# A decode layer with a cached attention window: maxima and mask added to the scores by VectorE instead of by two 512-column products, and key copies taken in turn

## The chip, the cores and the metric

The kernel runs on one core of one Trainium2 chip. The metric is the time of one execution on the device in microseconds (us); lower is better. Before the change the median of three runs is 127.63 us (127.57 to 128.44).

The core has a matrix engine (TensorE, "PE" in the profile; its weight loads are listed as "PEld"), a vector engine (VectorE, "DVE"), a scalar engine (ScalarE, "ACT"), GpSimd ("POOL") and SyncE ("SP"), which here issues the loads. Each engine runs its own list of instructions in order and waits for others by semaphores. Products are written to PSUM, from which VectorE and ScalarE read.

## The reference

One new token for each of 8 sequences goes through a layer norm, and then through attention over a cached window and through a gated feed-forward block. All inputs are bf16. The shapes are those of the inputs: x is 8 x 512, the caches 8 sequences x 8 key heads x 4096 positions x 128, of which the last W = 1024 are used.

```python
xn = _layernorm(x)
q  = (xn @ wq)                     # 512 -> 32 heads x 128, 4 query heads to a key head
k, v = k_cache[:, :, Sk - W:], v_cache[:, :, Sk - W:]        # W = 1024
scores = einsum("bhqd,bhkd->bhqk", q, k) * 128 ** -0.5
o  = einsum("bhqk,bhkd->bhqd", softmax(scores), v)
s  = o.reshape(8, 1, 32 * 128) @ wo                          # -> 512
g  = silu((gelu(xn @ w_gate) * (xn @ w_up)) @ w_down)        # 512 -> 1792 -> 512
return x + s * g
```

The bulk of the data are the keys and values: 64 pairs of a sequence and a key head, each 1024 x 128 in keys and again in values, 33.6 MB of the 47.5 MB read.

## The kernel before, in words

**Stages.** First the loads are issued; then come the layer norm, the feed-forward block and the query projection, which fill the first 33 us; then attention with the output projection in it; then the gate, the sum and the store. In the first stage `keep_busy` (L233) puts idle products between the pieces of work.

**Loads.** All large loads are issued by SyncE, in the order of L163 to L177, into a ring of 16 buffers of 1 MB: the feed-forward weights, the query weights, the first two key sets, and then for each q the key set q + 2, the value set q, and after every second q a slice of the output weights. A load waits until its buffer in the ring has been read.

**Rounds.** A round, numbered q from 0 to 15, takes QG = 4 sequences b..b+3 of one key head: a key set and a value set of 1 MB each. A load (L117) puts the 4 x 1024 keys of a set on 128 partitions in NCS = 32 chunks of 128 keys. Every chunk holds keys of all four sequences, 32 each, and the sequence of a row is its partition modulo 4. All 128 keys of a chunk are multiplied with the 16 queries of the four sequences (QC = 16 = 4 sequences x 4 query heads), and what belongs to another sequence has to be masked away. A round is worked in four quarters of 8 chunks, i from 0 to 3, and the quarters of all rounds are numbered g = 4 q + i. The small constants `row_of` (4 x 128, which row is whose) and `other` (4 x 16, -1e30 for the queries of the other sequences, else 0) make that mask as a product with 4 rows.

**The steps of a quarter or round** (all names and lines are of the kernel before):
- `transposes(g)` (L363): 8 transpositions of 128 x 128 keys into one PSUM tile `kT_ps` (two of these exist), and copies into SBUF: columns 0 to 639 by VectorE into `kTa` (L375), columns 640 to 1023 by ScalarE into `kTb` (L377).
- `scores(g)` (L381): in the first quarter of a round the mask is written into the whole score tile `sc_ps` (128 x 512 fp32, one product of 512 columns, L386). Then 8 products of 16 columns add the scores (L397).
- `max_keys(q)` (L406): the maximum over the 32 chunks, per partition and query, by VectorE (L408).
- `max_all(q)` (L413): the 128 x 16 maxima are transposed by PE (L416, fp32), reduced and negated by VectorE (L418), and put on the diagonal of a 48 x 16 bf16 tile `diag` in two parts, a value and its rounding rest (L423, L426).
- `exponentials(q)` (L436): a product of ones with this tile, 512 columns (L437), adds minus the maxima to the scores in PSUM; ScalarE takes the exponential into `pT` (L446).
- `sums(q)` (L448), `values(g)` (L469) and `normalise(q)` (L485): the sums over positions by 8 products with ones, reduced and inverted by VectorE; 8 products per quarter of the values with `pT`; and the result times the inverted sum into `oT_all` (L487).
- `project(h)` (L498): 4 products of the output weights of one head.

**Order.** There is no planner; the order of every engine is that of the program's text, the loop at L512 to L535. In step (q, i) PE does the transpositions of the next quarter, the maxima of the round before (at i = 1), the scores of this quarter, the sums (at i = 0) and values of the round two before, the exponentials of the round before (at i = 2), and in every second round, at i = 2 and 3, the projection of two heads each. At a round's end come `normalise` of the round two before and `max_keys` of this one. The tail, after the last quarter's scores, has no transpositions and scores left.

Of the kernel before, what the change touches and what calls it, by code (L numbers as in the profile page):

```python
# [17 lines left out]
def kernel(  # L18
# [30 lines left out]

    nc = tc.nc
    ctx.enter_context(tc.manual_schedule())

# [4 lines left out]
    W = min(4096, max(256, Sk // 4))  # L59
    win0 = Sk - W  # L60
    F = B_w_gate.shape[1]
    P = nc.NUM_PARTITIONS
    NDC = D // P
    NFC = F // P
    NSC = W // P
    UPK = NDC // 2
    DNJ = NFC // 2
    inv_sqrt_dh = float(Dh) ** -0.5

    QG = 4  # L70
    NB = QG
    NCS = QG * NSC
    VC = 4
    AC = 3
    NRING = 16
    MASK = -1.0e30
    NG = Hkv * B
    NQ = NG // QG
    QC = QG * rep
# [3 lines left out]
    consts = ctx.enter_context(tc.tile_pool(name="consts", bufs=1))  # L83
# [3 lines left out]
    ring = ctx.enter_context(tc.tile_pool(name="ring", bufs=NRING))  # L87
    kT_pool = ctx.enter_context(tc.tile_pool(name="kT_pool", bufs=3))
    p_pool = ctx.enter_context(tc.tile_pool(name="p_pool", bufs=4))
    small = ctx.enter_context(tc.tile_pool(name="small", bufs=2))  # L90
    ps_misc = ctx.enter_context(tc.tile_pool(name="ps_misc", bufs=1, space=PSUM))
    ps_kT = ctx.enter_context(tc.tile_pool(name="ps_kT", bufs=2, space=PSUM))
    ps_sc = ctx.enter_context(tc.tile_pool(name="ps_sc", bufs=2, space=PSUM))
    ps_mx = ctx.enter_context(tc.tile_pool(name="ps_mx", bufs=1, space=PSUM))
# [77 lines left out]
    for q in range(NQ):  # L172
# [12 lines left out]
        out=ident,  # L185
        in_=ident,
# [22 lines left out]
    other = consts.tile([QG, QG, rep], BF16, name="other")  # L209
    nc.vector.memset(other, MASK)  # L210
    nc.gpsimd.affine_select(
        out=other,
        in_=other,
# [3 lines left out]
        pattern=[[1, QG], [0, rep]],  # L217
        channel_multiplier=-1,
    )

    LO = 32
    diag = []
    for i in range(2):
        t = consts.tile([LO + QC, QC], BF16, name=f"diag{i}")
        nc.vector.memset(t, 0.0)
        diag.append(t)
    eps_sb = consts.tile([B, 1], FP32, name="eps_sb")
    nc.vector.memset(eps_sb, 1e-5)

# [3 lines left out]
    def keep_busy(n):  # L233
# [12 lines left out]
        out=rstd, in_=mv[:, 1:2], func=ACT.Sqrt, bias=eps_sb, scale=1.0  # L246
# [4 lines left out]
        out=xhat,  # L251
        in0=x_sb,
        scalar1=mv[:, 0:1],
        scalar2=rstd[:, 0:1],
        op0=ALU.subtract,
        op1=ALU.mult,
# [90 lines left out]
    for k in range(NDC):  # L347
        for m in range(Hq):
# [4 lines left out]
                start=(k == 0 and m == 0),  # L353
                stop=(k == NDC - 1),
                skip_group_check=True,
# [2 lines left out]
    nc.vector.tensor_copy(out=qT_all, in_=qT_ps.rearrange("p h b -> p b h"))  # L358


    kT, sc, pT, mxs, shift, recip = {}, {}, {}, {}, {}, {}

    def transposes(g):  # L363
        q, i = divmod(g, NB)
        kT_ps = ps_kT.tile([P, W], BF16, name="kT_ps")
        for c in range(NSC):
            n = i * NSC + c
            nc.tensor.transpose(  # L368
                kT_ps[:, c * P : (c + 1) * P],
                k_sb[q][:, n * Dh : (n + 1) * Dh],  # L370
                ident,
            )
        own = (NSC - AC) * P
        ta = kT_pool.tile([P, own], BF16, name="kTa")
        nc.vector.tensor_copy(out=ta, in_=kT_ps[:, 0:own])  # L375
        tb = kT_pool.tile([P, W - own], BF16, name="kTb")
        nc.scalar.copy(out=tb, in_=kT_ps[:, own:])  # L377
        kT[g] = [ta[:, c * P : (c + 1) * P] for c in range(NSC - AC)]
        kT[g] += [tb[:, c * P : (c + 1) * P] for c in range(AC)]

    def scores(g):  # L381
        q, i = divmod(g, NB)
        hkv, b = divmod(q * QG, B)
        if i == 0:
            sc[q] = ps_sc.tile([P, NCS, QC], FP32, name="sc_ps")
            nc.tensor.matmul(  # L386
                sc[q],
                row_of.rearrange("g e s -> g (e s)"),
                other.rearrange("g s j -> g (s j)")
                .unsqueeze(1)  # L390
                .to_broadcast([QG, NCS, QC]),
                start=True,
                stop=False,
                skip_group_check=True,
            )
        for c in range(NSC):
            nc.tensor.matmul(  # L397
                sc[q][:, i * NSC + c, :],
                kT[g][c],
                qT_all[:, b : b + QG, hkv * rep : (hkv + 1) * rep],  # L400
                start=False,
                stop=False,
                skip_group_check=True,
            )

    def max_keys(q):  # L406
        mx = small.tile([P, QC], FP32, name="mx")
        nc.vector.tensor_reduce(  # L408
            out=mx, in_=sc[q].rearrange("p c n -> p n c"), axis=AX.X, op=ALU.max
        )  # L410
        mxs[q] = mx

    def max_all(q):  # L413

        mxT_ps = ps_mx.tile([QC, P], FP32, name="mxT_ps")
        nc.tensor.transpose(mxT_ps, mxs[q], ident_f)  # L416
        nm = small.tile([QC, 1], FP32, name="nm")
        nc.vector.tensor_reduce(  # L418
            out=nm, in_=mxT_ps, axis=AX.X, op=ALU.max, negate=True
        )  # L420
        eye = ident_f[0:QC, 0:QC]
        parts = diag[q % 2]
        nc.vector.tensor_scalar(  # L423
            out=parts[0:QC, :], in0=eye, scalar1=nm[:, 0:1], scalar2=None, op0=ALU.mult
        )
        nc.vector.scalar_tensor_tensor(  # L426
            out=parts[LO : LO + QC, :],
            in0=eye,
            scalar=nm[:, 0:1],
            in1=parts[0:QC, :],  # L430
            op0=ALU.mult,
            op1=ALU.subtract,
        )
        shift[q] = parts

    def exponentials(q):  # L436
        nc.tensor.matmul(  # L437
            sc[q],
            ones_pp[0 : LO + QC, :],
            shift[q].unsqueeze(1).to_broadcast([LO + QC, NCS, QC]),  # L440
            start=False,
            stop=True,
            skip_group_check=True,
        )
        pT[q] = p_pool.tile([P, NCS, QC], BF16, name="pT")
        nc.scalar.activation(out=pT[q], in_=sc[q], func=ACT.Exp, scale=inv_sqrt_dh)  # L446

    def sums(q):  # L448
        sums_ps = ps_sum.tile([P, NB, QC], FP32, name="sums_ps")
# [60 lines left out]


    transposes(0)  # L512
    for q in range(NQ + LAG):
        v = q - LAG
        for i in range(NB):
            g = q * NB + i
            if g + 1 < NG:
                transposes(g + 1)
            if i == 1 and 1 <= q <= NQ:
                max_all(q - 1)  # L520
            if g < NG:
                scores(g)
            if v >= 0:
                if i == 0:
                    sums(v)
                values(v * NB + i)
            if i == 2 and 1 <= q <= NQ:
                exponentials(q - 1)
            if v >= SH and v % SH == 0 and i >= NB // 2:
                for h in range(2):  # L530
                    project((v // SH - 1) * rep + (i - NB // 2) * 2 + h)
        if v >= 0:
            normalise(v)
        if q < NQ:
            max_keys(q)  # L535
# [42 lines left out]
```

## Time and profile before

| | us |
|---|---|
| median of 3 runs | 127.63 (127.57 to 128.44) |
| the profiled execution, its own time | 127.63 |
| its span in the profile | 125.8 |
| PE busy in the span | 114.7 |
| VectorE busy | 64.5 |
| ScalarE busy | 42.5 |
| chain that ended last: PE's share | 73% |
| data read from HBM | 47.46 MB, 377 GB/s over the span |

The span runs from the first to the last instruction that the profile records; the execution's own time is 1.8 us more. A "busy" engine is one that has an instruction under way. Products overlap: a product that is listed with 0.2 us is followed by the next one after 0.03 to 0.06, so the time for which an instruction holds PE is read from the start of one to the start of the next, or from the chain, and not from its mean duration. The chain that ended last goes back from the last instruction to what released it, step by step, and gives the path that set the end. The slices cut the span in 40 parts of 3.1 us. The issue rows tell when a load is put on the queue; the median from there to its landing is 18.6 to 18.8 us for the keys and values.

### The profile page before, as it was taken

The numbers are of one execution on the slowest core, as the hardware profiler recorded it, in microseconds if no ns is written. First come the engines' busy times: TensorE is split into PE (matmuls) and PEld (weight loads), VectorE is DVE, ScalarE is ACT, GpSimd is POOL, SyncE is SP. The second block draws the span as 40 slices with busy tenths as digits, with TensorE's granted clock in tenths as the row PEclk, the third lists the DMA queues.
The fourth block names the chain that finished last, engine by engine and source line by source line (L and its number), as shares of the span: only waits on it lengthen the run. The fifth ranks groups of instructions, "written<-read, shape, count | busy, mean of one in ns | idle before, by whom it ended". The sixth has DMA issues, their size and how long they took to land.

```text
span 125.8 us, 4887 instructions
## 1 busy us (share of the span) xinstructions
PE 114.7 (91%) x2197; PEld 89.6 (71%) x2202; DVE 64.5 (51%) x200; ACT 42.5 (34%) x86; POOL 1.2 (1%) x7
## 2 busy tenths in 40 slices
PE   5899999989989999999999898989999999988780
PEld 1366663657777788887888787878787877877570
DVE  5200003010248768756786664858667677765531
ACT  4000005000054644543534254354544435352210
POOL 3000000000000000000000000000000000000000
PEclk9999999999999999999999999999999999999999
DMA  4999999999999999999999999999999999998300
GB/s 89 410 431 417 429 412 417 419 432 427 417 414 398 427 417 417 402 421 435 412 398 431 419 401 424 412 417 412 413 435 410 411 432 411 407 411 357 135 5 3
DMA packets 10325, 47.78 MB, mean 380 GB/s; under 512 B 816, under 2 KB 4928, under 8 KB 5696
## 3 DMA queue, kind: packets, MB, share of 16 engines
q1 hardware_dynamic: 10288, 47.46, 92.5%
q8 instruction: 17, 0.28, 0.9%
q14 instruction: 4, 0.03, 0.1%
q10 hardware_dynamic: 16, 0.01, 0.0%
HBM read 47.46 MB, written 0.01 MB: 377 GB/s over the span
## 4 chain that ended last, share of the span: by engine, by line
PE 73%; DVE 9%; ACT 6%; issue 5%; DMA 4%; ACTq 0%; DVEq 0%
PE kT_ps L368 19%; PE idle_ps L235 12%; PE o_ps L476 10%; PE sc_ps L397 9%; DVE kTa L375 6%; ACT kTb L377 6%; PE gu_ps L274 5%; DMA ring_sb<-in_B_w_gate_dram 4%; PE sc_ps L437 4%; PE sc_ps L386 4%; PE sT_ps L502 3%; PE sums_ps L451 3%; PE qT_ps L349 3%; PE fT_ps L313 1%; DVE mx L408 0%
## 5 line engine op out<-in xcount | busy, mean ns | idle before, releaser
L377 ACT COPY kTb<-kT_ps 128x384 bf16<-128x384 bf16 x64 | 30.6, 479 | 52.6 <-DVE kTa L375 52.6
L375 DVE COPY kTa<-kT_ps 128x640 bf16<-128x640 bf16 x64 | 31.3, 489 | 20.7 <-PE kT_ps L368 20.3
L368 PE MATMUL kT_ps<-ident,ring_sb 128*128 128x128 bf16 x512 | 39.1, 219 | 0.2 <-issue 0.2
L368 PEld LDWEIGHTS <-ring_sb 128*128 128x128 bf16 x512 | 29.4, 97 | 2.4 <-issue 2.2
L476 PE MATMUL o_ps<-pT,ring_sb 128*128 128x64 bf16 (+1 forms) x512 | 25.2, 190 | 2.2 <-issue 2.2
L235 PE MATMUL idle_ps<-ones_w 128*128 128x512 bf16 x53 | 20.0, 521 | 2.2 <-DVE ones_w L181 1.5
L476 PEld LDWEIGHTS <-ring_sb 128*128 128x128 bf16 x512 | 19.1, 97 | 3.0 <-issue 2.8
L397 PE MATMUL sc_ps<-qT_all,kTa 128*128 128x16 bf16 x320 | 17.8, 171 | 0.0
L397 PEld LDWEIGHTS <-kTa 128*128 128x128 bf16 x320 | 14.7, 96 | 4.2 <-issue 2.3
L397 PE MATMUL sc_ps<-qT_all,kTb 128*128 128x16 bf16 x192 | 14.5, 171 | 1.6 <-ACT kTb L377 0.4
L235 PEld LDWEIGHTS <-ones_w 128*128 128x128 bf16 x58 | 6.0, 121 | 8.8 <-issue 6.1
L397 PEld LDWEIGHTS <-kTb 128*128 128x128 bf16 x192 | 9.3, 96 | 3.3 <-ACT kTb L377 1.0
L408 DVE TENSOR_REDUCE mx<-sc_ps 128x16 f32<-128x512 f32 x16 | 10.9, 681 | 0.0
L446 ACT ACTIVATE pT<-sc_ps 128x512 bf16<-128x512 f32 x16 | 9.6, 601 | 2.7 <-PE sc_ps L437 2.6
L274 PEld LDWEIGHTS <-ring_sb 128*128 128x128 bf16 x112 | 7.4, 162 | 2.2 <-issue 1.6
L274 PE MATMUL gu_ps<-xnT_sb,ring_sb 128*128 128x8 bf16 x112 | 7.3, 201 | 0.5 <-DMA ring_sb<-in_B_w_gate_dram 0.5
L291 DVE TENSOR_SCALAR z<-z 128x112 f32<-128x112 f32 x1 | 0.2, 219 | 13.7 <-ACT z L288 13.7
L437 PE MATMUL sc_ps<-diag,ones_pp 48*128 48x512 bf16 x16 | 6.2, 386 | 0.4 <-DVE diag L426 0.4
L451 PE MATMUL sums_ps<-pT,ones_pp 128*128 128x64 bf16 x128 | 6.3, 192 | 0.0
L386 PE MATMUL sc_ps<-other,row_of 4*128 4x512 bf16 x16 | 6.2, 385 | 0.0
L502 PEld LDWEIGHTS <-wo_sb 128*128 128x128 bf16 x128 | 4.3, 96 | 2.5 <-issue 2.5
L502 PE MATMUL sT_ps<-oT_all,wo_sb 128*128 128x8 bf16 x128 | 5.4, 167 | 0.3 <-DVE oT_all L487 0.3
(54 smaller groups left out, 59.4 us busy)
## 6 DMA issues: line engine op xcount, KB each, us to landing
ring_sb<-in_A_k_cache_dram SPq DMA_DIRECT2D x16, 1024.0 KB, 18.8
ring_sb<-in_A_v_cache_dram SPq DMA_DIRECT2D x16, 1024.0 KB, 18.6
ring_sb<-in_A_wq_dram SPq DMA_DIRECT2D x4, 1024.0 KB, 19.5
wo_sb<-in_A_wo_dram SPq DMA_DIRECT2D x8, 512.0 KB, 17.8
ring_sb<-in_B_w_gate_dram SPq DMA_DIRECT2D x2, 896.0 KB, 5.0
ring_sb<-in_B_w_up_dram SPq DMA_DIRECT2D x2, 896.0 KB, 8.4
ring_sb<-in_B_w_down_dram SPq DMA_DIRECT2D x2, 896.0 KB, 12.9
x_sb<-in_A_x_dram ACTq DMA_DIRECT2D x1, 8.0 KB
```

What stands on the lines that cost most here:

```text
L235: nc.tensor.matmul(idle_ps, ones_w[:, 0:P], ones_w, start=True, stop=True)
L274: nc.tensor.matmul(ffn["gu"][:, j, n % 2, :], up_sb[n][:, i, j::NFC], xnT_sb[:, k, :], start=(n == 0 and j == 0 and i == 0), stop=(k == ND ...
L368: nc.tensor.transpose(kT_ps[:, c * P : (c + 1) * P], k_sb[q][:, n * Dh : (n + 1) * Dh], ident,)
L375: nc.vector.tensor_copy(out=ta, in_=kT_ps[:, 0:own])
L377: nc.scalar.copy(out=tb, in_=kT_ps[:, own:])
L386: nc.tensor.matmul(sc[q], row_of.rearrange("g e s -> g (e s)"), other.rearrange("g s j -> g (s j)") .unsqueeze(1) .to_broadcast([QG, NCS, ...
L397: nc.tensor.matmul(sc[q][:, i * NSC + c, :], kT[g][c], qT_all[:, b : b + QG, hkv * rep : (hkv + 1) * rep], start=False, stop=False, skip_g ...
L408: nc.vector.tensor_reduce(out=mx, in_=sc[q].rearrange("p c n -> p n c"), axis=AX.X, op=ALU.max)
L437: nc.tensor.matmul(sc[q], ones_pp[0 : LO + QC, :], shift[q].unsqueeze(1).to_broadcast([LO + QC, NCS, QC]), start=False, stop=True, skip_gr ...
L451: nc.tensor.matmul(sums_ps, ones_pp, pT[q][:, c * NB : (c + 1) * NB, :], start=(c == 0), stop=(c == NSC - 1),)
L476: nc.tensor.matmul(o_ps[q][:, 0:wide, :], v_sb[q][:, n * Dh : (n + 1) * Dh], pT[q][:, n : n + wide, :], start=(n == 0), stop=(n == NCS - 1 ...
L502: nc.tensor.matmul(sT_ps[0][:, d, :], wo_sb[:, h, d * P : (d + 1) * P], oT_all[:, h, :], start=(h == 0 and d == 0), stop=(h == Hq - 1), sk ...
```

## The change

Scores are no longer masked and shifted inside PSUM. The 512-column mask product goes from `scores`, whose products now each start anew. The maximum per partition is taken over unmasked scores; then `max_all` turns it with a plain fp32 product and adds the mask to the 16 x 128 result by a small product. A new function, `shift_all`, spreads the negated maxima over the 128 partitions with an fp32 product, adds the mask by a second small one, and copies the 128 x 16 result to SBUF; VectorE adds it to the 128 x 512 scores and writes the sum to SBUF, where the exponential reads it. The diagonal tiles and the 512-column product with them are gone. The keys of a quarter are copied whole, by VectorE for even i and by ScalarE for odd i. In the loop the value products stand ahead of the scores, and the three steps of the round before stand behind the scores at i = 0, 1 and 2.

```diff
     def transposes(g):
...
-        own = (NSC - AC) * P
-        ta = kT_pool.tile([P, own], BF16, name="kTa")
-        nc.vector.tensor_copy(out=ta, in_=kT_ps[:, 0:own])
-        tb = kT_pool.tile([P, W - own], BF16, name="kTb")
-        nc.scalar.copy(out=tb, in_=kT_ps[:, own:])
...
+        kT[g] = kT_pool.tile([P, W], BF16, name="kT")
+        if i % 2 == 0:
+            nc.vector.tensor_copy(out=kT[g], in_=kT_ps)
+        else:
+            nc.scalar.copy(out=kT[g], in_=kT_ps)

     def scores(g):
...
-            nc.tensor.matmul(
-                sc[q],
-                row_of.rearrange("g e s -> g (e s)"),
-                other.rearrange("g s j -> g (s j)")
-                .unsqueeze(1)
-                .to_broadcast([QG, NCS, QC]),
-                start=True,
-                stop=False,
-                skip_group_check=True,
-            )
...
-                start=False,
-                stop=False,
-                skip_group_check=True,
+                start=True,
+                stop=True,

     def max_all(q):
...
-        nc.tensor.transpose(mxT_ps, mxs[q], ident_f)
+        nc.tensor.matmul(mxT_ps, mxs[q], ident_f, start=True, stop=False)
+        nc.tensor.matmul(
+            mxT_ps,
+            other.rearrange("g s j -> g (s j)"),
+            row_of.rearrange("g e s -> g (e s)"),
+            start=False,
+            stop=True,
+        )
         nm = small.tile([QC, 1], FP32, name="nm")
         nc.vector.tensor_reduce(
             out=nm, in_=mxT_ps, axis=AX.X, op=ALU.max, negate=True
         )
-        eye = ident_f[0:QC, 0:QC]
-        parts = diag[q % 2]
-        nc.vector.tensor_scalar(
-            out=parts[0:QC, :], in0=eye, scalar1=nm[:, 0:1], scalar2=None, op0=ALU.mult
-        )
-        nc.vector.scalar_tensor_tensor(
...
-        shift[q] = parts
+        shift[q] = nm
+
+    def shift_all(q):
+
+        nm_ps = ps_mx.tile([P, QC], FP32, name="nm_ps", tag="mxT_ps")
+        nc.tensor.matmul(
+            nm_ps,
+            shift[q].to_broadcast([QC, P]),
+            ident_f[0:QC, 0:QC],
+            start=True,
+            stop=False,
+        )
+        nc.tensor.matmul(
+            nm_ps,
+            row_of.rearrange("g e s -> g (e s)"),
+            other.rearrange("g s j -> g (s j)"),
+            start=False,
+            stop=True,
+        )
+        to_add = small.tile([P, QC], FP32, name="to_add")
+        nc.vector.tensor_copy(out=to_add, in_=nm_ps)
+        shifted[q] = s_pool.tile([P, NCS, QC], FP32, name="shifted")
+        nc.vector.tensor_tensor(
+            out=shifted[q],
+            in0=sc[q],
+            in1=to_add.unsqueeze(1).to_broadcast([P, NCS, QC]),
+            op=ALU.add,
+        )

     def exponentials(q):
-        nc.tensor.matmul(
-            sc[q],
-            ones_pp[0 : LO + QC, :],
-            shift[q].unsqueeze(1).to_broadcast([LO + QC, NCS, QC]),
...
-        nc.scalar.activation(out=pT[q], in_=sc[q], func=ACT.Exp, scale=inv_sqrt_dh)
+        nc.scalar.activation(
+            out=pT[q], in_=shifted[q], func=ACT.Exp, scale=inv_sqrt_dh
+        )
...
             if g + 1 < NG:
                 transposes(g + 1)
-            if i == 1 and 1 <= q <= NQ:
-                max_all(q - 1)
-            if g < NG:
-                scores(g)
             if v >= 0:
                 if i == 0:
                     sums(v)
                 values(v * NB + i)
-            if i == 2 and 1 <= q <= NQ:
-                exponentials(q - 1)
+            if g < NG:
+                scores(g)
+            if 1 <= q <= NQ:
+                if i == 0:
+                    max_all(q - 1)
+                elif i == 1:
+                    shift_all(q - 1)
+                elif i == 2:
+                    exponentials(q - 1)
```

More of the change, by code (lines that the diff above doesn't have):

```diff
@@ L73 @@
     VC = 4
-    AC = 3
     NRING = 16
@@ L89 @@
     p_pool = ctx.enter_context(tc.tile_pool(name="p_pool", bufs=4))
+    s_pool = ctx.enter_context(tc.tile_pool(name="s_pool", bufs=2))
     small = ctx.enter_context(tc.tile_pool(name="small", bufs=2))
@@ L219 @@
     )
[L221 to L226, printed above, removed]
     eps_sb = consts.tile([B, 1], FP32, name="eps_sb")
@@ L358 @@
     nc.vector.tensor_copy(out=qT_all, in_=qT_ps.rearrange("p h b -> p b h"))
-    kT, sc, pT, mxs, shift, recip = {}, {}, {}, {}, {}, {}
+    kT, sc, pT, mxs, shift, shifted, recip = {}, {}, {}, {}, {}, {}, {}
     def transposes(g):
@@ L372, in transposes @@
             )
-        own = (NSC - AC) * P
-        ta = kT_pool.tile([P, own], BF16, name="kTa")
-        nc.vector.tensor_copy(out=ta, in_=kT_ps[:, 0:own])
-        tb = kT_pool.tile([P, W - own], BF16, name="kTb")
-        nc.scalar.copy(out=tb, in_=kT_ps[:, own:])
-        kT[g] = [ta[:, c * P : (c + 1) * P] for c in range(NSC - AC)]
-        kT[g] += [tb[:, c * P : (c + 1) * P] for c in range(AC)]
+        kT[g] = kT_pool.tile([P, W], BF16, name="kT")
[3 more added lines that the diff above has]
+            nc.scalar.copy(out=kT[g], in_=kT_ps)
     def scores(g):
@@ L398, in scores @@
                 sc[q][:, i * NSC + c, :],
-                kT[g][c],
+                kT[g][:, c * P : (c + 1) * P],
                 qT_all[:, b : b + QG, hkv * rep : (hkv + 1) * rep],
-                start=False,
-                stop=False,
-                skip_group_check=True,
+                start=True,
+                stop=True,
             )
@@ L420, in max_all, with exponentials @@
         )
-        eye = ident_f[0:QC, 0:QC]
-        parts = diag[q % 2]
-        nc.vector.tensor_scalar(
-            out=parts[0:QC, :], in0=eye, scalar1=nm[:, 0:1], scalar2=None, op0=ALU.mult
-        )
-        nc.vector.scalar_tensor_tensor(
[L427 to L432, printed above, removed]
-        )
-        shift[q] = parts
-    def exponentials(q):
+        shift[q] = nm
[7 more added lines that the diff above has]
+            stop=False,
+        )
         nc.tensor.matmul(
-            sc[q],
-            ones_pp[0 : LO + QC, :],
-            shift[q].unsqueeze(1).to_broadcast([LO + QC, NCS, QC]),
+            nm_ps,
+            row_of.rearrange("g e s -> g (e s)"),
+            other.rearrange("g s j -> g (s j)"),
             start=False,
             stop=True,
-            skip_group_check=True,
         )
+        to_add = small.tile([P, QC], FP32, name="to_add")
[7 more added lines that the diff above has]
+        )
+    def exponentials(q):
         pT[q] = p_pool.tile([P, NCS, QC], BF16, name="pT")
-        nc.scalar.activation(out=pT[q], in_=sc[q], func=ACT.Exp, scale=inv_sqrt_dh)
+        nc.scalar.activation(
+            out=pT[q], in_=shifted[q], func=ACT.Exp, scale=inv_sqrt_dh
+        )
     def sums(q):
```

## The prediction

> **What bounds the kernel now.** I read the page's slices first, then the chain of work that ended last, then the timeline. Two rows of the slices:
>
> ```profile
> PE 114.7 (91%) x2197; PEld 89.6 (71%) x2202; DVE 64.5 (51%) x200; ACT 42.5 (34%) x86; POOL 1.2 (1%) x7
> ...
> PEclk9999999999999999999999999999999999999999
> DMA  4999999999999999999999999999999999998300
> ```
>
> The loads run full from the second slice to the 36th, with nothing left to fill, and the matrix engine (PE) is busy beside them at its full clock. Which is later is read from the issue rows of the loads and the PE timeline. The last loads are issued at:
>
> ```profile
> 90.76 1.91 SPq L117 DMA_DIRECT2D ring_sb<-in_A_k_cache_dram  x1
> 93.25 1.86 SPq L117 DMA_DIRECT2D ring_sb<-in_A_v_cache_dram  x1
> ...
> 98.22 3.04 SPq L117 DMA_DIRECT2D ring_sb<-in_A_v_cache_dram  x2
> ```
>
> With the median of 18.6 to 18.7 us from issue to landing, the last key set (round 15) lands at 109.5 and value set 13 at 111.9. PE starts to transpose that key set at 110.2 and to use those values at 112.6. So at the end PE is only 0.7 us behind the loads; at round 3 (issued 20.3, so landed about 39.0; transposed from 46.1) it was 7 behind. PE sets the pace and the loads stand just ahead of it: a slower PE shows in full, a faster one gains less than a microsecond.
>
> The pace of PE, from the chain, round 3 (a round is one key set, one value of q, worked in four quarters):
>
> ```profile
> 47.47 0.32 PE sc_ps L386
> 47.79 0.29 PE sc_ps L397 x8
> 48.08 0.25 PE sums_ps L451 x8
> 48.33 0.23 PE o_ps L476 x8
> 48.56 0.46 PE kT_ps L368 x8
> ...
> 50.39 0.25 PE o_ps L476 x8
> 50.64 0.32 PE sc_ps L437
> ```
>
> From this mask product (L386) to the next at 52.38 it is 4.91 us, with PE busy for 4.86. Rounds with the output projection (every second one, 16 more products) take 5.3 to 5.5, and several have 0.3 to 0.5 of "issue" gaps in the midst of a group of products. These gaps wait for no engine in the trace; I leave them as they are.
>
> **The change, part by part, per round.**
>
> Removed from PE: the two 512-column products, 0.32 each on the chain (63.21 - 62.89 for L386), 0.64. The transposition of the maxima (L416) held PE from 59.42 to 59.53, 0.11. Together 0.75.
>
> The Trainium skill, "TensorE: Matmul & The Clock Gate", section "Back-to-back issue gap", gives N/2.4 + 2.5 ns, 216 ns for 512 columns. By that estimate only 0.43 + 0.11 would be removed and the body below would come out 2.7 us longer. The row (0.32, reload of the next weights included) decides.
>
> Added to PE: an fp32 product of the maxima with the identity, which is no transposition any more (128 columns, 16-column weights), a 128-column bf16 mask product, an fp32 product of the negated maximum (128-column weights, 16 columns) and a 16-column mask product. The bf16 pair costs as its neighbours: 0.06 for 128 columns (0.46 / 8, L368) and 0.04 for 16 (0.29 / 8, L397). No row shows a plain fp32 product. The nearest is the fp32 transposition, also 128 columns:
>
> ```profile
> 59.42 0.27 PE L416 MATMUL mxT_ps<-ident_f,mx 128*16 128x128 f32 x1
> 59.53 0.22 PE L397 MATMUL sc_ps<-qT_all,kTa 128*128 128x16 bf16 x3
> ```
>
> It occupied 0.11, twice a bf16 one (0.06). Least: the product costs as much as that, 0.11, and the 16-column one as a bf16 score, 0.04; with the masks 0.25. Most: four passes of 0.11, and four weight loads at the 0.12 of L235's load plus 0.04 each; with masks 0.44 + 0.64 + 0.10 = 1.18. I take two passes: 0.22, and two weight loads of 0.12 that hide nothing, with the columns and masks 0.38 in all, so 0.60. I choose it because the transposition, with one pass of fp32 at 0.11, is the nearest row, and both halves of two numbers have to go through.
>
> The same page of the skill (section "Terms") says that the transpose mode is 4 times faster for FP32. By it, as an estimate, the first product alone would be 0.44 and the sum 0.82; no row of the trace shows the pair, and the time would be 3 us longer.
>
> Key copies: VectorE took 640 columns, then ScalarE 384 of the same tile, one after the other:
>
> ```profile
> L377 ACT COPY kTb<-kT_ps 128x384 bf16<-128x384 bf16 x64 | 30.6, 479 | 52.6 <-DVE kTa L375 52.6
> L375 DVE COPY kTa<-kT_ps 128x640 bf16<-128x640 bf16 x64 | 31.3, 489 | 20.7 <-PE kT_ps L368 20.3
> ```
>
> From a tile's last transposition to its last copy was 0.02 + 0.50 + 0.08 + 0.49 + 0.05 = 1.14 (44.11 to 45.25). Whole copies: VectorE from the line through 174 ns at 32 columns (L263) and 489 at 640, 0.69; ScalarE from 198 ns at 32 columns (L325) and 479 at 384, 0.99, or 1.01 by the slope to 601 at 512. With 0.2 ahead and 0.05 behind, an even quarter's copy takes 0.94 and an odd one's 1.27. Since the value products now stand ahead of the scores, PE has, between the last transposition of a quarter and its scores, at least values 0.25, scores 0.29, transpositions 0.46, values 0.25 = 1.25. So the odd copies are hidden but for 0.02, and exactly at the edge: each 0.1 more there costs 0.1 in a round without projection.
>
> VectorE: out go two diagonal operations (0.22 each) and 4 x 0.49; in come 2 x 0.69, a small copy (0.17) and the addition over 512 fp32 from PSUM (the reduction L408 of that size takes 0.68, a two-operand row of 112 takes 0.27, which scales to 0.69). 3.60 busy in a round becomes about 3.5: no bound. ScalarE: 4 x 0.48 + 0.60 = 2.5 becomes 2 x 1.01 + 0.60 = 2.6, off the bound. The loads' queue and its order are untouched.
>
> New waits: the maxima's product now waits for the maximum in the open. Counting from the end of a round's first transpositions: copy 0.2 to 0.89, normalisation to 1.15, maximum 1.18 to 1.86, product at 1.91; PE gets there at 0.25 + 0.29 + 0.46 + 0.25 + 0.25 + 0.29 = 1.79. A stall of 0.12, with the next transpositions queued behind it. In rounds with projection 0.29 more work lies in between, and this stall and the 0.02 are gone. The second fp32 product waits for the negated maximum, 0.27 + 0.25 after the first; transpositions, values and scores (1.0) cover it.
>
> Body: 4.91 - 0.75 + 0.60 + 0.14 = 4.90 without projection; with it 5.5 - 0.15 = 5.35. Over the 13 rounds from 2 to 15 that is no change, to -0.9; I take 0 because of gaps that a hand count doesn't see.
>
> Start: in the first two rounds there are no values to cover the copies. Stepping through with 0.69, 1.01, 0.46 and 0.29: the scores of quarter 1 wait for ScalarE until 35.63, those of quarter 3 until 37.65, the first shift is ready at 41.5, and round 2's second transpositions start at 42.36 where they now start at 41.95. +0.4.
>
> End: from the last transposition of the last quarter (115.0) to the maximum at 117.16 was 2.13; now the copy on ScalarE 1.27, scores 0.29 + 0.17 to land, 0.03: 1.76, as the normalisation no longer stands in between. -0.4. From the start of the maximum to the last exponential was 2.31 (117.16 to 119.47). Now: maximum 0.73 with its hop, fp32 product and mask 0.49 (0.32 before, plus 0.17), reduction 0.33, second product and mask 0.48, small copy 0.22, addition 0.74 = 2.99. +0.7.
>
> Sum: 0 + 0.4 - 0.4 + 0.7 = +0.7. Span 125.8 + 0.7 = 126.5. The profiled execution took 127.63, 1.8 beyond its span, and equals the median of the runs shown: **128.3 us**. One per cent (1.3 us) is about what can be told from no change.
>
> **Rivals.**
>
> 1. Dear fp32 products (slower). Place: the two products in PE's queue, in every round. Price: each 0.1 over 0.60 is 1.3 us in the body and 0.1 in the tail; from about 0.65 it is over 128.9, and at 0.89, midway between my choice and the most, it is 0.29 x 14 = 4.1 more, 132.4. For it: nothing in the trace shows a plain fp32 product, and PE has nothing to give. Against: fp32 needs twice, not four times, in the one row there is. At the most (1.18) it would be 136.
>
> 2. The loads decide (X, the added PE time of a round, under 0.45). Then PE catches up and waits for value set 13 at 111.9: two groups of values (0.50), two of scores (0.58), two of transpositions (0.92) and both new pairs of products (0.3) later the last quarter's keys are transposed, at 114.2, 0.8 earlier than now, and the late start no longer counts. 125.8 - 0.8 - 0.4 + 0.6 = 125.2, so 127.0; with the least X 0.1 less. It can't go much below, so faster by 1% has little behind it: it would need the copies' chaining to have cost PE more than the 0.05 a round that it is not busy.
>
> 3. VectorE as the bound: if the addition (0.69) or the small copy comes before a key copy that is due, each round loses up to 0.3; 14 x 0.3 = 4.2, 132.5. Against: the first product's reduction, copy, addition and next copy end 0.4 ahead of need by the count above.
>
> 4. The whole copies free PE more than counted (the scores no longer wait for the second half, 0.15 in a step of the chain): up to 0.15 x 13 = 2 us, but capped by the loads at 126.9.
>
> **Chances.** Forecast (X 0.45 to 0.70, 127.0 to 129.7) 0.49, of which 0.08 is over 128.9; rival 1 0.29; rival 2 0.12; rival 3 0.05; rival 4 0.05, of which 0.02 under 126.4. Faster by over 1% 0.02, with 0.01 for what I don't see 0.03; slower 0.08 + 0.29 + 0.05 = 0.42; same 0.55. Range: 126.9, where the loads hold it, to 132.4, which leaves out the dearer half of rivals 1 and 3 (0.17).
>
> **What would show it.** The rows of the fp32 products: number of passes, and how long PE is held until the next product. The round without projection: 4.9 if right, 5.2 or more under rival 1. No wait of PE for a key copy worth more than 0.05 a round, a small one for the maximum. Round 2 some 0.4 later. Start of the last maximum to its exponential 3.0. DMA share falling in the last slices as now; if it falls in the midst, the ring is held up by PE. What makes the prediction wrong first is the price of the fp32 products, then a stall at the edge of ScalarE's copy.

## The result and the profile after

The changed kernel is slower. Over 20 runs of each its median is 129.69 us against 127.47 us; the ratio is 1.0153, with a 95% interval of 1.0116 to 1.0191, which is 1.95 us. This ratio leaves out the runs that are more than 1.5% above the fastest of their kernel, so it is smaller than the ratio of the two medians, 1.0174. The median lies in the range of the prediction (126.9 to 132.4), 1.4 over its value (128.3). The outcome is "slower by over 1%", which had a chance of 0.42, against 0.55 for no change.

The profiled execution of the changed kernel took 130.63 us. It ran at half of PE's clock for 3.4 us in the middle and again at the end, which not every execution does; the experiments come back to that. Its page, rows 1 and 2, cut to the rows shown of before:

```profile
PE 116.0 (90%) x2250; PEld 95.4 (74%) x2250; DVE 63.8 (50%) x166; ACT 44.6 (35%) x54; POOL 1.2 (1%) x7
...
PEclk9975556999999999999999999959999999999755
DMA  3999999999999999999999999999999999983000
```

The loads end where they did (the last packet lands at 118.3 us, before at 119.0). The page lists 53 more products of PE and 48 more weight loads than before; 5 of the 53 are idle products of the first stage, of which the page of before lists 53 for 58 weight loads. The clock row has a 5 in the 27th slice and 7, 5, 5 at the end, where before had only nines. (The 7, 5, 5, 5, 6 near the start fall in the first stage.)

The groups of the costliest instructions that the prediction turned on:

```profile
L372 ACT COPY kT<-kT_ps 128x1024 bf16<-128x1024 bf16 x32 | 32.4, 1012 | 52.9 <-PE kT_ps L363 51.9
...
L370 DVE COPY kT<-kT_ps 128x1024 bf16<-128x1024 bf16 x32 | 22.1, 692 | 19.4 <-PE kT_ps L363 18.0
...
L398 PE MATMUL mxT_ps<-ident_f,mx 128*16 128x128 f32 x32 | 6.3, 278 | 0.2 <-DVE mx L390 0.2
...
L415 PE MATMUL nm_ps<-ident_f,nm 16*128 16x16 f32 x32 | 6.2, 268 | 0.0
```

The copies last 1.01 and 0.69 us as reckoned. Each fp32 product is listed twice a round (x32 in 16 rounds): two passes. What they hold of PE is read in PE's timeline, from start to start:

```profile
58.22 0.39 PE L398 MATMUL mxT_ps<-ident_f,mx 128*16 128x128 f32 x2
58.54 0.22 PE L399 MATMUL mxT_ps<-row_of,other 4*16 4x128 bf16 x1
58.69 0.62 PE L363 MATMUL kT_ps<-ident,ring_sb 128*128 128x128 bf16 x8
...
59.66 0.39 PE L415 MATMUL nm_ps<-ident_f,nm 16*128 16x16 f32 x2
59.90 0.16 PE L422 MATMUL nm_ps<-other,row_of 4*128 4x16 bf16 x1
60.00 0.28 PE L363 MATMUL kT_ps<-ident,ring_sb 128*128 128x128 bf16 x2
```

The first pair holds PE for 0.32 + 0.15, the second for 0.24 + 0.10: 0.81 a round, where I had taken 0.60. And yet, in the chain, a round without projection takes what it took before:

```profile
47.19 0.23 PE sums_ps L448 x8
...
47.84 0.32 PE mxT_ps L398 x2
48.16 0.15 PE mxT_ps L399
...
49.28 0.32 PE nm_ps L415 x2
...
52.09 0.23 PE sums_ps L448 x8
```

From sums to sums it is 4.90, against 4.91 before and 4.90 in the prediction. The next round, with projection and without a gap, takes 5.13 (5.31 before). So the loss is not in a round without gaps. The experiments look for it.

### The profile page after: what moved, and what is told of

Its sections match the earlier page's. It is cut to its first block, busy times and chain, and to the rows that moved or that the text cites. A ratio compares the mean times of both kernels' runs of the same rounds, so it can differ in the third digit from the quotient of the medians.

```text
span 128.9 us, 4919 instructions
## 1 busy us (share of the span) xinstructions
PE 116.0 (90%) x2250; PEld 95.4 (74%) x2250; DVE 63.8 (50%) x166; ACT 44.6 (35%) x54; POOL 1.2 (1%) x7
## 4 chain that ended last, share of the span: by engine, by line
PE 84%; issue 4%; DMA 4%; DVE 3%; ACT 3%; DVEq 0%
PE kT_ps L363 25%; PE o_ps L473 12%; PE idle_ps L230 12%; PE sc_ps L380 10%; PE gu_ps L269 5%; PE mxT_ps L398 4%; PE nm_ps L415 4%; DMA ring_sb<-in_B_w_gate_dram 4%; PE sums_ps L448 3%; PE qT_ps L344 3%; PE sT_ps L499 2%; PE mxT_ps L399 2%; ACT kT L372 2%; DVE kT L370 1%; PE fT_ps L308 1%
## 5 line engine op out<-in xcount | busy, mean ns | idle before, releaser
L372 ACT COPY kT<-kT_ps 128x1024 bf16<-128x1024 bf16 x32 | 32.4, 1012 | 52.9 <-PE kT_ps L363 51.9
L370 DVE COPY kT<-kT_ps 128x1024 bf16<-128x1024 bf16 x32 | 22.1, 692 | 19.4 <-PE kT_ps L363 18.0
L380 PE MATMUL sc_ps<-qT_all,kT 128*128 128x16 bf16 x512 | 22.9, 170 | 3.2 <-issue 1.6
L380 PEld LDWEIGHTS <-kT 128*128 128x128 bf16 x512 | 18.0, 96 | 4.9 <-issue 1.9
L390 DVE TENSOR_REDUCE mx<-sc_ps 128x16 f32<-128x512 f32 x16 | 10.9, 684 | 0.9 <-PE sc_ps L380 0.8
L432 DVE TENSOR_TENSOR shifted<-sc_ps,to_add 128x512 f32<-128x512 f32 x16 | 11.1, 692 | 0.6
L441 ACT ACTIVATE pT<-shifted 128x512 bf16<-128x512 f32 x16 | 10.1, 633 | 3.2 <-DVE shifted L432 3.2
L407 DVE TENSOR_REDUCE nm<-mxT_ps 16x1 f32<-16x128 f32 x16 | 4.5, 279 | 6.2 <-PE mxT_ps L399 6.2
L398 PE MATMUL mxT_ps<-ident_f,mx 128*16 128x128 f32 x32 | 6.3, 278 | 0.2 <-DVE mx L390 0.2
L448 PEld LDWEIGHTS <-ones_pp 128*128 128x128 bf16 x128 | 5.6, 101 | 1.0 <-issue 1.0
L415 PE MATMUL nm_ps<-ident_f,nm 16*128 16x16 f32 x32 | 6.2, 268 | 0.0
```

Source lines behind the costliest of these rows:

```text
L370: nc.vector.tensor_copy(out=kT[g], in_=kT_ps)
L372: nc.scalar.copy(out=kT[g], in_=kT_ps)
L380: nc.tensor.matmul(sc[q][:, i * NSC + c, :], kT[g][:, c * P : (c + 1) * P], qT_all[:, b : b + QG, hkv * rep : (hkv + 1) * rep], start=True ...
L390: nc.vector.tensor_reduce(out=mx, in_=sc[q].rearrange("p c n -> p n c"), axis=AX.X, op=ALU.max)
L398: nc.tensor.matmul(mxT_ps, mxs[q], ident_f, start=True, stop=False)
L415: nc.tensor.matmul(nm_ps, shift[q].to_broadcast([QC, P]), ident_f[0:QC, 0:QC], start=True, stop=False,)
```

## The experiments

Three theories were there at the start. PACE: PE's own work sets the pace of the rounds. TAIL: the loss lies behind the last transposition. EDGE: the whole copies hold PE up. After the first four runs a fourth was formed, SUPPLY: under the loads PE gets its instructions too slowly. All ratios are to the kernel before, run beside it on the same chip (r5 to r8 on another chip than the rest).

### r1_changed: the changed kernel again

> The changed kernel again, beside the kernel before on one chip, for a base that the other runs of this call share. All theories: ratio 1.010 to 1.020, time near 129.4 us. Theory PACE (PE's own work sets the pace of a round, and the fp32 products hold it 0.81 us a round where I took 0.60) and theory TAIL (the rounds are no longer than before, 4.90 against 4.91 us, and the loss lies behind the last transposition: a longer chain and a halved clock of PE there) differ in the profile: by PACE round 15's transpositions start 0.5 us or more later than before, by TAIL at most 0.3 later and the stretch from the last transposition to the store is over 1 us longer than the 8.4 us of before.

Ratio 1.0182 (1.0123 to 1.0242). Its profiled execution ran at full clock from the first stage up to 4.4 us before the store, which makes it the better one to compare. Stage by stage, with windows cut at the first transposition, the second and the last maximum (start of L408 or L390), the last exponential and the store. The columns are the window, its length, and the busy time and number of PE's products, of PE's weight loads, of VectorE, ScalarE and GpSimd, then PE's clock, the loads' share and GB/s. Before:

```profile
33.45:42.19 8.74, 8.26 (x146) 6.76 (x145) 5.43 (x13) 4.18 (x9) 0.00 (x0) 1.00 1.02 414
42.19:117.16 74.97, 71.47 (x1589) 60.41 (x1587) 51.21 (x155) 34.13 (x71) 0.00 (x0) 1.00 1.01 412
117.16:119.47 2.31, 1.74 (x38) 1.27 (x38) 1.74 (x7) 0.00 (x0) 0.00 (x0) 1.00 0.28 101
119.47:123.42 3.95, 2.87 (x84) 2.48 (x83) 1.54 (x6) 0.60 (x1) 0.00 (x0) 1.00 0.02 4
```

The changed kernel in this run:

```profile
33.71:42.65 8.94, 7.68 (x147) 6.45 (x146) 5.11 (x9) 4.50 (x5) 0.00 (x0) 1.00 1.02 416
42.65:118.59 75.94, 70.59 (x1628) 63.97 (x1626) 50.33 (x125) 35.75 (x43) 0.00 (x0) 1.00 0.99 404
118.59:121.70 3.11, 2.85 (x62) 2.24 (x62) 2.25 (x7) 0.08 (x1) 0.00 (x0) 1.00 0.02 5
121.70:126.80 5.10, 3.35 (x60) 2.90 (x59) 1.41 (x6) 0.63 (x1) 0.00 (x0) 0.57 0.00 0
```

Four things are to be seen. The start costs 0.2. The rounds cost 0.97, although PE is busy for 0.88 us less in them: it has become idler by 1.85. From the last maximum to the exponential it is 0.8 more. And from there to the store it is 1.15 more, at a mean clock of 0.57. The forecast had asked when the transpositions of round 15 start: at 111.43 us against 110.24, 1.2 later, which is what PACE expected (0.5 or more) and not TAIL (0.3 at most). But PACE's reason does not hold, as PE has less to do in the rounds and not more. From the last transposition to the store it is 9.9 us against 8.4, as TAIL expected. Neither says why PE idles in the rounds.

The idle stretches of PE in the rounds are named "issue": they wait for no engine. They last 0.4 to 0.8 us each, where before they lasted 0.2 to 0.6, and each stands in the midst of a group:

```profile
94.90 0.20 PE L473 MATMUL o_ps<-pT,ring_sb 128*128 128x64 bf16 x1 [0.77 <-issue]
100.82 0.40 PE L363 MATMUL kT_ps<-ident,ring_sb 128*128 128x128 bf16 x4 [0.45 <-issue]
```

### r2_bf16_maxima: the price of the fp32 products

```diff
-        mx = small.tile([P, QC], FP32, name="mx")
+        mx = small.tile([P, QC], BF16, name="mx")
...
-        nc.tensor.matmul(mxT_ps, mxs[q], ident_f, start=True, stop=False)
+        nc.tensor.matmul(mxT_ps, mxs[q], ident, start=True, stop=False)
...
-        nm = small.tile([QC, 1], FP32, name="nm")
+        nm = small.tile([QC, 1], BF16, name="nm")
...
-            ident_f[0:QC, 0:QC],
+            ident[0:QC, 0:QC],
```

> The changed kernel with the maxima and the negated maximum kept in bf16, so that both fp32 products become bf16 products of one pass (any common shift leaves the softmax as it is). PACE: the added PE time of a round falls from 0.81 to about 0.3, 0.5 x 13 = 6 us less for PE, of which the loads let through some 1 us, and 0.4 less in the last chain: 1.4 us under the changed kernel, ratio to before 1.004. TAIL: only the last chain's 0.4 us: 129.0, ratio 1.012. Loads as the limit: value set 13 still waited for, the last transpositions not before 114.2 us.

Ratio 1.0014 (0.9950 to 1.0078), 2.1 us under the changed kernel; PACE had 1.4 and TAIL 0.4. The size of this gain is rough: the twelve runs go from 126.6 to 131.6 us, and the medians of all runs are 1.6 apart. A round without projection and without a gap took 4.53 instead of 4.90, so the fp32 products do cost PE 0.4 a round more than the same products in bf16. But in the waits of PE the gaps grew:

```profile
PE o_ps L473 <- issue: 2.9, 5, 1.1
PE sc_ps L380 <- issue: 1.1, 1, 1.1
PE sT_ps L499 <- issue: 0.9, 1, 0.9
PE kT_ps L363 <- issue: 0.8, 1, 0.8
PE sums_ps L448 <- issue: 0.6, 1, 0.6
```

Together they are 6.3 us, against 4.8 in the run above: a PE with less to do waits longer for the same thing.

### r3_split_copies: the copies as before

The edit puts the two copies of before back into `transposes` and keeps all the rest of the change.

> The changed kernel with the key copies as before, 640 columns by VectorE and then 384 by ScalarE. Theory EDGE (ScalarE's whole copy of 1.01 us makes PE wait for the odd quarters and holds up the last chain, and its queue puts the last exponentials but one behind the last copy): 1 to 2 us under the changed kernel. PACE and TAIL: the chain of two copies is 1.14 us, 0.13 less than ScalarE's 1.27, so 0.1 less in the last stretch, the sums of round 14 no longer wait (0.3), the body the same: 0.2 to 0.5 us less. VectorE's queue is then fuller by 0.6 us a round (4.1 of 4.9), which could cost 0.1 a round.

Ratio 1.0274 (1.0223 to 1.0325): 1.2 us slower than the changed kernel, not faster. A round without projection takes 5.09 to 5.16 in the first rounds, and the waits of PE have a row for the copies, which the changed kernel does not have inside the rounds:

```profile
PE sc_ps L382 <- ACT kTb L372: 1.2, 5, 0.3
```

EDGE is wrong: the split copies are the ones that come too late. The likely reason is that VectorE now also adds the shift (it is busy for 57.5 us between the second and the last maximum, against 50.3 in r1); this was not tried alone.

### r4_double_fp32: the fp32 product of the maxima twice

```diff
         nc.tensor.matmul(mxT_ps, mxs[q], ident_f, start=True, stop=False)
+        nc.tensor.matmul(mxT_ps, mxs[q], ident_f, start=False, stop=False)
```

> The changed kernel with the fp32 product of the maxima done twice, added up (a shift twice as large leaves the softmax as it is). PACE: 0.27 to 0.32 more PE time in each round, 13 rounds, 3.5 to 4.2 us and 0.3 in the last chain: 133.3. TAIL, with slack in the rounds before the loads: under 1 us more, 130.2.

Ratio 1.0265 (1.0197 to 1.0332), 1.1 us over the changed kernel. PACE had 3.5 to 4.2, TAIL under 1; the intervals of r4 and r1 overlap. In the two profiles PE's busy time between the second and the last maximum rose by 3.2 us, and the stretch itself by 1.4.

What the gaps are is told by the records of single DMA packets. The page of every run lists, beside the loads, a queue of kind "instruction"; for the kernel before:

```profile
q8 instruction: 17, 0.28, 0.9%
```

These are 17 packets of 16 KB, and 0.28 MB is 64 bytes for each of PE's 4,400 instructions: one packet carries 256 of them. In the kernel before 13 such packets start from 43.32 to 116.94 us, one in 6.1 us; in r1 from 43.62 to 116.09, in r2 from 42.36 to 115.37, in r4 from 43.57 to 116.42: 6.0, 6.1 and 6.1. In the first stage, with PE at few instructions, two came 15 us apart, and at the end, with the loads done, two came 3.4 to 3.8 apart.

The gaps stand where the packets end. From the end of one gap to the end of the next PE of r1 has 128 products and 128 weight loads, 256 instructions, though the gaps stand in the midst of different groups (three windows, each cut 10 ns ahead of a gap's end):

```profile
76.85:82.77 5.92, 5.34 (x128) 4.89 (x128) 3.59 (x9) 2.55 (x3) 0.00 (x0) 1.00 1.02 427
100.81:107.01 6.20, 5.58 (x128) 5.11 (x128) 4.17 (x10) 3.00 (x4) 0.00 (x0) 1.00 1.01 422
107.01:113.20 6.19, 5.35 (x128) 4.90 (x128) 4.13 (x11) 2.56 (x4) 0.00 (x0) 1.00 1.03 412
```

In the kernel before and in r1, r2, r4, r6 and r7 every such gap of the rounds ends 1.2 to 1.6 us after a packet has landed, and a whole multiple of 256 instructions after the gap before it. A fixed price that PE pays for each instruction, the obvious rival, would not gather in one place; nor is it there where PE has its instructions: the round of 5.13 us above has 252 of them, 20 ns each.

So from the first gap on the rounds take a packet's 6.1 us for each 256 instructions, which is 6.1 / 256 = 0.024 us an instruction. The change removes 6 of PE's instructions from a round (two wide products and a transposition, each with its weight load) and adds 12 (two fp32 products of two passes, two mask products). The next three runs test this on the kernel before.

### r5_merged_sums: fewer instructions, the same columns

```diff
-        sums_ps = ps_sum.tile([P, NB, QC], FP32, name="sums_ps")
-        for c in range(NSC):
+        wide = 4 * NB
+        sums_ps = ps_sum.tile([P, wide, QC], FP32, name="sums_ps")
+        for c in range(2):
             nc.tensor.matmul(
                 sums_ps,
                 ones_pp,
-                pT[q][:, c * NB : (c + 1) * NB, :],
+                pT[q][:, c * wide : (c + 1) * wide, :],
                 start=(c == 0),
-                stop=(c == NSC - 1),
+                stop=(c == 1),
             )
```

> The kernel before, with the sums over positions as 2 products of 256 columns instead of 8 of 64 (12 fewer instructions of PE in a round, the same columns; VectorE reduces 256 instead of 64, 0.41 against 0.22 us). Theory SUPPLY (under the loads PE gets its instructions in blocks of 16 KB, 256 of them, one about every 6.1 us, and this paces the rounds; 0.024 us an instruction): 12 x 14 x 0.024 = 4.0 us less for PE, of which the loads let through some 0.8: ratio 0.993, the gaps called issue in the midst of groups longer than before while PE stands ahead, the last transposition at 114.2 us. Theory PACE (PE's own work): the time of PE is the same, ratio 1.000 to 1.003.

Ratio 0.9942 (0.9903 to 0.9981), where SUPPLY had 0.993. One forecast of it was wrong: the issue gaps did not grow, they went. The waits of PE in the rounds are now for the loads:

```profile
PE kT_ps L368 <- DMA ring_sb<-in_A_k_cache_dram: 2.0, 2, 1.1
PE sc_ps L397 <- ACT kTb L377: 0.2, 1, 0.2
PE o_ps L477 <- DMA ring_sb<-in_A_v_cache_dram: 0.2, 1, 0.2
```

### r6_tiny_pairs and r7_wide_product: instructions against work

Both add work of no use to each round, ahead of the sums and into their PSUM tile, which is widened for it: r6 eight products of 8 columns, r7 one of 512 (the edits are cut to the added products).

```diff
+        for c in range(8):
+            nc.tensor.matmul(
+                sums_ps[:, NB, 0:8], ones_pp, pT[q][:, c, 0:8], start=True, stop=True
+            )
```

```diff
+        nc.tensor.matmul(sums_ps, ones_pp, pT[q], start=True, stop=True)
```

> The kernel before, with 8 more products of 8 columns a round ahead of the sums, each with its weight load, of no use to the result: 16 instructions and 0.29 us of PE more in a round. SUPPLY: 16 x 14 x 0.024 = 5.4 us more, 132.8. PACE: 0.29 x 14 = 4.1 us more, 131.4. Theory LOADS (the last loads set the end whatever PE does): under 1 us more.

> The kernel before, with one more product of 512 columns a round ahead of the sums, of no use to the result: 2 instructions and 0.32 us of PE more in a round. SUPPLY: 2 x 14 x 0.024 = 0.7 us more plus what of the 0.32 does not fit into the gaps (0.1 a round): 1 to 2 us more, 128.9. PACE: 0.32 x 14 = 4.5 us more, 131.8. Against the run with 8 small pairs: by SUPPLY a good deal less, by PACE slightly more.

r6: median 132.79 us, ratio 1.0403 (1.0333 to 1.0473). r7: 128.69 us, 1.0086 (1.0042 to 1.0130). SUPPLY had 132.8 and 128.9; PACE had 131.4 and 131.8. In r6 PE's listed busy time between the second maximum and the last grows by 4.0 us and the stretch by 5.0; in r7 the busy time grows by 2.4 and the stretch by 0.8. So a microsecond of work in 16 instructions a round lengthens the stretch by 1.25, and in 2 instructions by 0.36. In the first two full rounds, ahead of any gap, the two take the same, 5.11 and 5.13 us against 4.91: there PE's own work still sets the pace. The first gap stands at 58.8 us in the kernel before and in r6, at 70.4 in r1 and at 77.3 in r7. The whole list, from a window of each run as above (instructions are products and weight loads together, as listed):

| run | PE's instructions | PE products busy, us | stretch, us | ns an instruction |
|---|---|---|---|---|
| before | 3176 | 71.47 | 74.97 | 23.6 |
| r1 changed | 3254 | 70.59 | 75.94 | 23.3 |
| r2 bf16 maxima | 3198 | 67.51 | 74.70 | 23.4 |
| r3 split copies | 3254 | 71.02 | 76.56 | 23.5 |
| r4 fp32 twice | 3310 | 73.82 | 77.33 | 23.4 |
| r6 tiny pairs | 3400 | 75.44 | 79.92 | 23.5 |
| r7 wide product | 3198 | 73.83 | 75.81 | 23.7 |
| r8 tail busy | 3254 | 70.58 | 75.39 | 23.2 |
| r12 copies in turn | 3170 | 69.95 | 75.17 | 23.7 |
| r5 merged sums | 3002 | 71.77 | 74.88 | 24.9 |
| r9 changed, merged sums | 3086 | 70.20 | 73.13 | 23.7 |
| r10 changed, all three | 3030 | 66.15 | 74.00 | 24.4 |
| r11 before, tuned | 2994 | 70.11 | 73.57 | 24.6 |

In the nine rows without the merged sums PE's busy time varies by 12%, the price of an instruction by 2%. r2 and r7 have the same number of instructions: PE of r7 is busy for 6.3 us more, and its stretch is 1.1 longer. With the merged sums the loads come in: r5 waited 2 us for them.

### r8_tail_busy: the clock at the end

```diff
+            if q == NQ and i in (0, 3):
+                tail_busy(2 if i == 0 else 3)
```

`tail_busy` does products of 512 columns into a free tile of `kT_ps`.

> The changed kernel with 2 and 3 idle products of 512 columns on PE in the last stretch, where it waits for VectorE (behind the last maxima's products, and ahead of the last sums). Theory CLOCK (the granted clock halves 5 to 8 us before the end because PE is idle too long there, and the stretch from the last exponential to the store takes 5.1 us instead of 4.0): the clock stays full to the end, that stretch is 4.0 us, and the median is 1 us under the changed kernel's 129.7 to 130.4; the fastest runs, which had no such halving, stay as they were (128.2 to 129). Without CLOCK: no change or 0.2 us more.

Median 128.91, ratio 1.0113 (1.0052 to 1.0173). The clock row and the two last stages (windows as above):

```profile
PEclk9985555999999999999999999999999999999996
```

```profile
116.99:120.42 3.43, 3.30 (x66) 2.48 (x66) 2.25 (x7) 0.07 (x1) 0.00 (x0) 1.00 0.19 65
120.42:124.42 4.00, 2.80 (x63) 2.05 (x61) 1.42 (x6) 0.63 (x1) 0.00 (x0) 0.99 0.00 0
```

From the last exponential to the store it is 4.00 instead of 5.10, at full clock. One profile would not be enough, as that of r3, without these products, also kept its clock to 0.7 us before the store. But the mean clocks of all executions agree: 5 us at half are 0.02 of the span, and of the 26 executions of the changed kernel in the result and r1, 18 lie at 0.90 to 0.925 or at 0.955 to 0.978, of the six of r8 none (0.936 to 0.942, and one at 0.993). So the cause named CLOCK is shown: with more for PE to do while VectorE and ScalarE work on the last shift, the clock is no longer halved for the last products. The seven executions of the result outside these two groups have a median of 128.9, as r8 has, and the fastest runs stay where they were, as forecast (128.28, against 128.20 in the result). The ratio falls by 0.7 points; the intervals overlap a little, so the size of the gain is not settled.

### r9_changed_merged and r10_changed_all: the change without its loss

r9 is the changed kernel with the edit of r5; r10 has the edits of r2, r5 and r8.

> The changed kernel with the sums as 2 products of 256 columns (12 fewer instructions of PE in a round). SUPPLY: the blocks of instructions no longer pace the rounds; the last transposition comes at 114.2 us, where the loads allow it, instead of 116.9, and what is left of the loss is the last stretch (maximum to exponential 3.1 against 2.3 us, and the halved clock in some executions): 2 us under the changed kernel, ratio to before 1.003. If the loss in the rounds was PE's own work or the copies, no change: 1.016.

> The changed kernel with all three: sums as 2 products, maxima in bf16, and the idle products in the last stretch. If the loss consists of supply of instructions, length of the last chain and halved clock, it is now gone but for 0.4 us of the chain, and the gain of the run with merged sums alone (ratio 0.994) is reached: 0.995 to 0.999, and above the next run.

r9: 127.90 us, ratio 1.0022 (0.9987 to 1.0057), forecast 1.003. The last transposition ends at 114.0, 2.9 earlier than in r1, and the last maximum to the exponential is 3.11 as there. So what the change loses in the rounds comes back when PE has fewer instructions, though the fp32 products are all still there. r10: 126.26 us, ratio 0.9906 (0.9874 to 0.9938), better than forecast, with ten runs between 126.06 and 126.42. Its PE now waits for the loads at six places:

```profile
PE kT_ps L363 <- DMA ring_sb<-in_A_k_cache_dram: 2.9, 4, 0.9
PE o_ps L474 <- DMA ring_sb<-in_A_v_cache_dram: 1.5, 2, 1.0
```

### r11_before_tuned: the kernel before without the limit

The kernel before with the edit of r5, the value products ahead of the scores as in the change, and the maxima and their transposition in bf16, so that one diagonal tile of 16 x 16 does and L426 goes.

> The kernel before with the sums as 2 products, the value products ahead of the scores, and the maxima in bf16 so that one diagonal tile does instead of two. The last transposition at 114 us as with merged sums alone; from there to the maximum 1.7 instead of 2.1 us, to the exponential 2.0 instead of 2.3: 0.7 us under the run with merged sums alone, 125.7, ratio 0.988. Value set 15 (landed 118.0) is then nearly the limit.

126.18 us, ratio 0.9916 (0.9880 to 0.9951), a little less gain than forecast. It can't be told apart from r10. Both beat the kernel before and the changed one.

### r12_turn_only: one part of the change alone

The kernel before with the copies in turn, nothing else.

> The kernel before with the key copies in turn alone. The count of PE's instructions is that of before, so by SUPPLY the rounds take the same; ScalarE's 1.27 us for an odd quarter fits the 1.3 to 1.6 us that PE needs between its transpositions and scores where the two wide products stand in between; the last copy ends 0.13 later. Ratio 0.998 to 1.004. If whole copies cost a wait in each round (theory EDGE): 1.01 or more.

126.84 us, ratio 0.9967 (0.9930 to 1.0004). This part costs nothing, and may gain 0.4 us.

## Why the prediction was right or wrong, point by point

**What bounds the kernel.** "PE sets the pace and the loads stand just ahead of it" is the step that failed. The loads stand where I put them (r5 and r10 run into them), and in the first rounds PE does set the pace; from 58.8 us on it was set by the supply of PE's instructions, at 23.2 to 23.7 ns each. The 4.91 us that I worked with held for three of the rounds without projection; the other four took 5.26 to 5.38. That the median lies in the range is in part luck: "slower" stood there for dear fp32 products, and what made it slower, the supply and the clock at the end, was in no term of the sum. The page had the trace of it, and I had it in hand: "These gaps wait for no engine in the trace; I leave them as they are." Eight gaps of 0.2 to 0.6 us in the rounds, 2.6 us in all, were the mark of the bound.

**The price of the fp32 products.** Two passes, as chosen, but 0.81 instead of 0.60 a round: 0.10 on the first (0.32 from start to start, against 0.22), behind which the mask's weights are loaded only with the mask's product, at 58.54, and not ahead of it, and 0.15 of the 0.21 for the two masks (0.25 against 0.10), less 0.04 on the second product. The Trainium skill, "TensorE: Matmul & The Clock Gate", "Terms", has the transpose mode 4 times faster for FP32; here a plain product of 128 columns held PE for 0.32 and the transposition for 0.11, 3 times.

**The round.** 4.90 was forecast and 4.90 measured, with two errors against each other: the products cost 0.21 more, and about as much was gained that I had left for rival 4; that it is the scores, which no longer wait for the second half of a copy, was not tried alone. PE is busy for 4.88 of the 4.90. With projection 5.35 was forecast, and 5.13 measured where no gap stood in the round. The price I put on rival 1, 1.3 us for each 0.1, was far too high: r4 raised PE's time by 3.2 us and the time by 1.1. Work is cheap while it fills gaps; instructions are not (r6 and r7). With 0.81 that price would have added 2.7 and given 131.

**The rounds together.** Forecast to the last maximum: 0 for the body and -0.4 for what the reordering saves there; measured +0.97 in r1 and +0.42 in r8. The 78 instructions more by 23.4 ns are 1.8 us, which with the -0.4 is 1.4: more than measured, of the right sign (in r1 the supply binds from 70.4 us on, before from 58.8, so not all 78 count in full). This term, taken as 0, is the mis-sized one.

**Start.** +0.4 forecast, +0.2 measured.

**End.** From the last transposition to the maximum 1.66 in r1 (1.76 forecast), to the exponential 3.11 (2.99). The halving of the clock behind it, 1.1 us in those executions that have it, was not in the prediction at all. Part of it I could have seen: I counted the removed wide products as gain only, and r8 shows what wide products in that stretch are worth.

**Copies and VectorE.** The whole copies took 1.012 and 0.692, the addition 0.692 (0.69 forecast), the exponential from SBUF 0.633 against 0.601 from PSUM, which I had not counted. No wait for a key copy in the rounds; one of 0.5 at the last quarter, and the sums of the last round but one wait 0.2 for their exponential, which stands behind the last copy in ScalarE's queue. Rival 3 did not come.

Summed up for an execution with full clock: 0.2 + (0.4 to 1.0) + 0.8 = 1.4 to 2.0 us, against 1.95 from the ratio, where I had 0.7.

## What to carry to other kernels

Where an engine shows small idle gaps at even distances, in the midst of groups and with nothing named as their cause, count its instructions from gap to gap before you count its work: if the count is constant (here 256), the stage costs a price per instruction, and an edit is to be judged by the instructions it adds or saves. Two wide products replaced by four short ones and their passes can then cost more than they free; eight products into one tile made two, with the same columns, gained 0.6% of the time. And a product that is taken out of the last stretch takes some of PE's activity with it: look at the clock row of the last slices.

## What the runs showed of the hardware

- PE's instructions arrive in packets of 16 KB, 256 instructions each, listed among the queues of the core's 16 DMA engines beside the loads. With the loads at full share one came every 6.0 to 6.2 us on the mean in every kernel that did not wait for the loads; this paced PE at 23.2 to 23.7 ns an instruction. In the kernel before and r1 a packet mostly starts 3.5 to 3.8 us after the end of the gap before, takes 1.0, and its first instruction runs 1.2 to 1.6 after it has landed. Why it takes so long was not tried: a run with fewer loads would tell whether the packets queue behind them. That two came 3.4 to 3.8 us apart once the loads had ended speaks for it, and 15 us apart in the first stage, when PE had few instructions, agrees with packets that are fetched as they are used up.
- The granted clock of PE fell to one half for the rest of the execution in the profiles of the changed kernel, r1, r2, r4 and r9, 4.4 to 6.0 us ahead of the store. In the 3.41 us before the fall PE was listed as busy for 2.60 us in r1 and for 2.90 in the first profile of the changed kernel; in the kernel before it was busy for 2.77 from 118.73 to 122.15 us, and the clock stayed full. So the listed busy time does not tell when the clock falls; what does is open. The Trainium skill, "TensorE: Matmul & The Clock Gate", "What's actually happening", lets the clock fall after an idle window of about 3.4 us; here it fell with PE listed as busy for three quarters of that time and more. The halved stretch in the middle of the profiled execution lasted 3.41 us, as that window.
- A plain fp32 product is listed as two products with a weight load each, and held PE 0.32 us for 128 columns and 16 weights, 0.24 for 16 columns and 128 weights.
- The kernel before itself spread from 126.3 to 129.7 us in its runs, and the kernels that are limited by the loads (r5, r10, r11) mostly within 0.4 us. What spreads the first is open.
